# Pairing the first unit's attention tiles into one series and delaying the operand mixing in a fused attention and maxout kernel on Trainium2

## The chip, the cores and the metric

The kernel runs on one core of one Trainium2 chip. The metric is the time of one execution in microseconds (us). The engines are named as in the profile: PE is TensorE, DVE is VectorE, ACT is ScalarE, POOL is GpSimd, SP is SyncE, whose queue issues nearly all DMAs here. PEld is PE's loading of stationary operands.

## The reference, cut to what matters

Chunked softmax attention (8 batches, 8 heads, 576 positions, 64 columns, chunks of 64), and behind it a layer of three matrix products of which the largest is kept, and an output product:

```python
scores = scale * np.matmul(q_c, k_c.transpose(0, 1, 2, 4, 3))
scores = scores - np.max(scores, axis=-1, keepdims=True)
attn = np.exp(scores)
attn = attn / (np.sum(attn, axis=-1, keepdims=True) + 1e-09)
out = np.matmul(attn, v_c)
...
h = np.maximum(np.maximum(x @ w1, x @ w2), x @ w3)   # x 4608x512, w 512x768
return (h @ w_out).astype(np.float32)                # w_out 768x512
```

All of it is float32; the kernel splits each operand of a product into a high and a low part and makes three products (`three`).

## The kernel before, in words

The 4608 rows are 36 tiles of 128. Tiles 0 to 3 are a first group, whose order is written out by hand (`FIRST`). Tiles 4 to 7 are a second group, with plain products. Tiles 8 to 35 are four units of 6, 8, 8 and 6 tiles (`UNITS`). Each unit has a hidden layer of nine sets of seven products each (a fast scheme that needs seven products of half size where eight would stand, in the order `ORDER` = 1, 6, 5, 7, 2, 3, 4), and an output layer (`project`) of 6 x 3 matmuls a tile. A product is six matmuls of 384 columns in units of 6 tiles and of 512 columns in units of 8. The weights of a set (1.75 MB) come back from DRAM into a ring of two places (`load`, two DMAs), where they were put, mixed, during the second group (`store`, `stores`, nine times).

Attention of a tile goes through these steps, named as in the code: q (load of q and k), S (scores, 64x64 matmuls on PE), mx and sub on DVE, exp on ACT, sum, eps, rec on DVE, nrm (the division), T (four transposes on PE), at (copy to SBUF on ACT), v (load), V (values, 64x64 matmuls on PE), x (copy on ACT into `stage`). The attention of a unit is made in the stage before it, and its steps are put between the matmuls there. A clock of planned time, `now`, is moved on by each product (`passed`), and a step planned for a time (`plan`) is issued as soon as `now` has come to it. So the order on each engine is fixed when the program is built, and an engine takes its instructions in that order, waiting at each for its data.

Before the change two ways of placing attention exist. For units 1 to 3 `insertion` takes tiles two by two: the V of one pair and the S of the next stand together on PE, with the offsets of `PAIR` and `PAIR_T`; V writes to two banks of PSUM out of the five that the products use (`take`, `give`), and nrm is on POOL. For the six tiles of the first unit, `attention` and `tiles` place each tile by itself during the second group, with the offsets of `TABLE` and `LATER`; S and V of these tiles write to the two halves of a bank of their own, and nrm is on DVE.

A unit's operands X1 to X7 are made from `stage` during the output layer of the stage before it (`operands`: a cast on ACT as the high part, a difference on DVE as the low part, and four mixing differences, two on DVE and two on POOL), at times counted from the end of the hidden layer, from 0.0 to 9.4, all moved by `OPERANDS`. In the output layer a tile's result is copied out of its bank by ACT (`output`). The parts H of the hidden layer that the output layer reads come from a cast on ACT and a difference on DVE (`high`, `low` of `hidden`); those of the last set are needed in the output layer after its first 36 matmuls and the first tile's next three.

Of the kernel before, what the change touches and what calls it, by code (L numbers as in the profile page):

```python
# [19 lines left out]
B, H, S, D = 8, 8, 576, 64  # L20
P = 128
# [7 lines left out]
STEP, TILE = 0.6815, 2.05  # L29
STEP_H = {6: 0.517, 7: 0.6003, 8: 0.6815}  # L30
ORDER = (1, 6, 5, 7, 2, 3, 4)
TABLE = (("q", -7.0, 0.0), ("v", -1.0, 0.0), ("S", 0.0, 0.7), ("mx", 1.0, 0.0), ("sub", 1.9, 0.0), ("exp", 2.8, 0.0),
         ("sum", 3.8, 0.0), ("eps", 4.7, 0.0), ("rec", 4.9, 0.0), ("nrm", 5.3, 0.0), ("T", 8.0, 0.65), ("at", 8.9, 0.0),
         ("V", 10.6, 0.7), ("x", 11.6, 0.0))
PAIR = (("mx", 1.4, 2.9), ("sub", 2.2, 3.7), ("exp", 3.1, 4.6), ("sum", 4.1, 6.0), ("eps", 5.0, 6.9), ("rec", 5.2, 7.1),
        ("nrm", 5.6, 7.5))
PAIR_T = (("T", 10.0, 12.4, 0.46), ("at", 10.9, 13.3, 0.0))
OPERANDS = 0.3
MIX = 0.5
LATER = {"q": -2.0, "v": 1.5, "T": 1.4, "at": 1.4, "V": 2.8, "x": 2.8}  # L40

# [26 lines left out]
def chunk_attn_maxout_kernel(  # L68
# [10 lines left out]
    nc = tc.nc  # L79
# [134 lines left out]
    def bank_of(name):  # L214
        if name not in banks_of:
            banks_of[name] = ps[name].tile([P, 2, 2, 4, 64], F32, name=name[-1])
        return banks_of[name]

    def plain_steps(t, x_of, col, paired=None):


        st = {}

        def load_qk():
            st["r"] = att.tile([P, 2, 8, 64], F32, name="buf", tag=("raw", "kk", "aa")[t % 3] if t < 8 else ("raw", "kk")[t % 2],
                               bufs=1)
            nc.sync.dma_start(out=st["r"], in_=qk[t])

        def load_v():
            st["v"] = att.tile([P, 8, 64], F32, name="buf", tag=f"vs{t % 2}", bufs=1)  # L230
            nc.sync.dma_start(out=st["v"], in_=vb[t])

        def scores():
            r = st["r"]
            st["s"] = s = bank_of("ps_s")[:, :, t % 2 if t < 4 or paired is not None else 0]
            for g in range(4):
                for h, c in quarters:
                    a, b = halves_of[c], halves_of[h]
                    nc.tensor.matmul(out=s[b, c, g, :], lhsT=r[a, 0, 2 * g + h, :], rhs=r[a, 1, 2 * g + h, :],  # L239
                                     start=True, stop=True)  # L240

        def maximum():
            st["mx"] = tmp.tile([P, 32], F32, name="mx")[:, :8]
            nc.vector.tensor_reduce(out=st["mx"].rearrange("p (g c) -> p c g", c=2), in_=st["s"], axis=AX.X, op=ALU.max)  # L244

        def less():
            st["e"] = ep.tile([P, 4, 2, 64], F32, name="e", tag=("et", "e")[t % 2])
            most = st["mx"].rearrange("p (g c) -> p c g", c=2)
            nc.vector.tensor_tensor(out=st["e"].rearrange("p g c k -> p c g k"), in0=st["s"],  # L249
                                    in1=most.unsqueeze(3).broadcast_to([P, 2, 4, 64]), op=ALU.subtract)  # L250

        def exp():
            nc.scalar.activation(out=st["e"], in_=st["e"], func=AF.Exp, scale=SCALE)

        def total():
            total, st["guard"], st["invert"], st["norm"] = over_sum(st["e"].rearrange("p g c k -> p (g c) k"))
            total()

        def transpose():
            st["tp"] = tp = ps_t.tile([P, 4, P], F32, name="tp")  # L260
            for g in range(4):
                nc.tensor.transpose(out=tp[:, g, :], in_=st["e"][:, g].rearrange("p c k -> p (c k)"),  # L262
                                    identity=ident)

        def transposed():
            st["at"] = xs_p.tile([P, 4, P], F32, name="xs")
            nc.scalar.copy(out=st["at"], in_=st["tp"])

        def values():
            if paired is not None:  # L270
                x = [p[:, t % 2] for p in paired["x"]]
            else:
                st["x"] = bank_of("ps_x")[:, :, t % 2] if t < 4 else bank_of("ps_s")[:, :, 1]
                x = [st["x"][:, c] for c in range(2)]
            for g in range(4):
                for h, c in quarters:
                    a, b = halves_of[c], halves_of[h]
                    nc.tensor.matmul(out=x[c][b, g, :], lhsT=st["v"][a, 2 * g + h, :], rhs=st["at"][a, g, b],  # L278
                                     start=True, stop=True)

        def part(x):
            return x[:, :, col:col + P].rearrange("p g (c x) -> p c g x", c=2)

        def high():
            nc.scalar.copy(out=part(x_of()[0]), in_=st["x"])

        def low():
            xh, xl = x_of()
            nc.vector.tensor_tensor(out=part(xl), in0=st["x"], in1=part(xh).bitcast(F32), op=ALU.subtract)  # L289

        def whole():
            nc.scalar.copy(out=part(x_of()), in_=st["x"])

        return dict(q=load_qk, v=load_v, x=whole, S=scores, mx=maximum, sub=less, exp=exp, sum=total,
                    eps=lambda: st["guard"](), rec=lambda: st["invert"](), nrm=lambda *eng: st["norm"](*eng),
                    T=transpose, at=transposed, V=values, xh=high, xl=low)

    begun = {}

    def attention(t, x_of, col, norm, later):  # L300
        steps = begun[t] if t in begun else plain_steps(t, x_of, col)
        step = steps["nrm"]
        steps["nrm"] = lambda: step(norm)
        return [(at + later.get(name, 0.0), pe, steps[name]) for name, at, pe in TABLE
                if not (t in begun and name == "q")]

    outputs = []

# [367 lines left out]
    def plan(at, pe, fn):  # L676
        heapq.heappush(due, (at, len(order), pe, fn))
        order.append(fn)
# [23 lines left out]
        units.append((unit(t0, count, rooms), t0, count))  # L702
        t0 += count

    def tiles(lead, time):
        _, t0, count = units[0]
        for tt in range(count):
            first = now + lead + (time - 13.5 - lead) * tt / (count - 1)
            for at, pe, fn in attention(t0 + tt, stage, tt * P, nc.vector, LATER):
                plan(first + at, pe, fn)  # L710

    pairs = []
    for _, t0, count in units[1:]:
        for n in range(0, count, 2):
            both = dict(col=n * P)
            both["tiles"] = [plain_steps(t0 + tt, stage, tt * P, both) for tt in (n, n + 1)]
            pairs.append(both)

    def value_banks(both):
# [12 lines left out]
    def insertion(when, k, behind=0.0):  # L732
# [8 lines left out]
        for n, steps in enumerate(scored):  # L741
            plan(when + 0.003 + 0.001 * n, 0.65, steps["S"])
            for name, *at in PAIR:
                fn = steps[name]
                plan(when + lead + at[n], 0.0, (lambda fn=fn: fn(nc.gpsimd)) if name == "nrm" else fn)
# [4 lines left out]
            for n, steps in enumerate(pairs[k + 1]["tiles"]):  # L750
                plan(when + 4.0 + n, 0.0, steps["q"])

    def series(u, time):

        done = sum(count // 2 for _, _, count in units[1:u + 1])
        if u + 1 >= len(units):
            return
        n = units[u + 1][2] // 2
        lead = 9.0
        if u == 0:  # L760
            for m, steps in enumerate(pairs[0]["tiles"]):
                plan(now - 4.0 + m, 0.0, steps["q"])
            plan_at = now + 4.0
            insertion(plan_at, 0)
            lead = 20.0
        for k in range(n):
            insertion(now + lead + (time - 3.5 - lead) * k / (n - 1), done + k + 1, 14.0 if k == n - 1 else 0.0)

# [10 lines left out]
    def operands(u):  # L779
        if u < len(units):  # L780
            for at, fn in units[u][0]["operands"]():
                plan(now + OPERANDS + at, 0.0, fn)

    def load(u, n, *at):
        if n >= len(sets):
# [2 lines left out]
            for t, fn in zip(at, units[u][0]["load"](n)):  # L788
                plan(now + t, 0.0, fn)

    inner = 3 * JT * CT * STEP + UNITS[0] * TILE
    parts += [("do", lambda: tiles(7.0, inner - 2.0))]
    parts += [("steps", lambda j=j, w=w: g["hidden"](j, w)) for j in range(JT) for w in range(3)]
    parts += [("do", change), ("do", lambda: operands(0)), ("do", lambda: load(0, 0, 0.0, 1.0)), ("do", lambda: load(0, 1, 2.0, 3.0))]
    parts += [("steps", lambda: g["project"](0, 1)), ("steps", lambda: g["project"](2)), ("steps", lambda: g["project"](3))]
    def units_of(u):
        return UNITS[u] if u < len(UNITS) else 0

    for u, (it, t0, count) in enumerate(units):
        time = len(sets) * 14 * STEP_H[count] + (units_of(u + 1) * 1.6)  # L800
        parts.append(("do", lambda u=u, time=time: series(u, time)))
        for n in range(len(sets)):
            parts.append(("steps", lambda it=it, n=n: it["hidden"](n)))
            parts.append(("do", lambda u=u, n=n: load(u, n + 2, 0.3, 0.9)))
# [56 lines left out]
```

## Time and profile before

| | |
|---|---|
| median of 3 runs | 637.86 us (637.18 to 639.95) |
| profiled execution | 637.51 us |
| its span, first to last instruction | 635.7 us |
| PE busy | 623.2 us, 98% of the span |
| DVE busy | 415.0 us, 65% |
| ACT busy | 233.9 us, 37% |
| POOL busy | 217.9 us, 34% |
| granted TensorE clock, mean | 1.000 |

Busy time of an engine is counted without its register, branch and semaphore instructions. The profiled execution's time is 1.8 us above its span. Matmuls are pipelined, so one begins before the one ahead of it ends: what a matmul costs is read from the distance of two starts and not from its own duration. The second group lasts from about 95.6 to 174.1 us, unit 0 to 283.2 us, unit 1 to 415.8 us, unit 2 to 541.9 us.

### The profile page before, as it was taken

How to read it: one execution, taken by the hardware profiler on the slowest of the kernel's cores; microseconds unless marked ns; L12 is line 12 of the kernel's file. 1: busy time of each engine (PE TensorE's matmuls, PEld its weight loads, DVE VectorE, ACT ScalarE, POOL GpSimd, SP SyncE). 2: the span in 40 equal slices, each digit the busy share in tenths (PEclk: the TensorE clock that was granted, in tenths of full speed). 3: DMA queues.
4: the chain of work that ended last, by engine and by line, in shares of the span. 5: the costliest groups of instructions: out<-in, count | busy, mean ns of one | idle time of the engine just before them, and what ended most of it. 6: DMA issues, size and time to landing. Idle time of an engine off the chain costs nothing.

```text
span 635.7 us, 12387 instructions
## 1 busy us (share of the span) xinstructions
PE 623.2 (98%) x5101; PEld 530.0 (83%) x5102; DVE 415.0 (65%) x661; ACT 233.9 (37%) x400; POOL 217.9 (34%) x186
## 2 busy tenths in 40 slices
PE   7899999999999999999999999999999999999997
PEld 4888878777899999788888888788888888999986
DVE  5889855886767676956767679336676690376530
ACT  4988633443424333442332324312223151122121
POOL 3423577882332233222332234213232350222210
PEclk9999999999999999999999999999999999999999
DMA  8978559763869774825474817227454162367502
GB/s 331 389 278 289 194 179 332 241 230 143 330 227 321 250 274 174 318 112 196 167 298 148 296 31 309 100 81 285 167 214 168 64 263 85 134 232 246 217 18 82
DMA packets 36055, 133.70 MB, mean 210 GB/s; under 512 B 4000, under 2 KB 6560, under 8 KB 30240
## 3 DMA queue, kind: packets, MB, share of 16 engines
q1 hardware_dynamic: 35856, 132.79, 56.7%
q8 instruction: 40, 0.66, 0.4%
q14 instruction: 15, 0.12, 0.1%
q10 hardware_dynamic: 144, 0.13, 0.1%
HBM read 106.95 MB, written 25.95 MB: 209 GB/s over the span
## 4 chain that ended last, share of the span: by engine, by line
PE 88%; DVE 8%; DMA 1%; POOL 1%; issue 1%; ACT 1%; SPq 0%; ACTq 0%; POOLq 0%; DVEq 0%
PE pm L189 27%; PE pm L190 26%; PE pm L191 26%; PE s L239 3%; PE tp L262 2%; PE pm L278 2%; DMA ring<-w 1%; PE s L278 1%; DVE X L465 1%; DVE most L525 1%; PE pm L638 1%; DVE e L249 1%; DVE sm L197 1%; DVE mx L244 1%; DVE kept L456 1%
## 5 line engine op out<-in xcount | busy, mean ns | idle before, releaser
L189 PE MATMUL pm<-X,ring 128*128 128x512 f32 (+1 forms) x504 | 185.4, 368 | 0.5 <-DVE most L525 0.3
L191 PE MATMUL pm<-X,ring 128*128 128x512 f32 (+1 forms) x504 | 182.5, 362 | 0.0
L190 PE MATMUL pm<-X,ring 128*128 128x512 f32 (+1 forms) x504 | 182.4, 362 | 0.0
L519 POOL TENSOR_TENSOR kept<-kept 128x384 f32<-128x384 f32 (+1 forms) x36 | 41.5, 1152 | 229.1 <-DVE kept L513 218.8
L513 DVE TENSOR_TENSOR kept<-pm,kept 128x384 f32<-128x384 f32 (+1 forms) x72 | 44.8, 622 | 110.6 <-PE pm L191 109.9
L189 PEld LDWEIGHTS pm<-X,ring 128*128 128x128 f32 x504 | 94.6, 188 | 11.5 <-DVE most L525 1.1
L191 PEld LDWEIGHTS pm<-X,ring 128*128 128x128 f32 x504 | 94.6, 188 | 10.0
L190 PEld LDWEIGHTS pm<-X,ring 128*128 128x128 f32 x504 | 94.7, 188 | 9.5
L510 ACT COPY kept<-pm 128x384 f32<-128x384 f32 (+1 forms) x72 | 38.4, 533 | 124.0 <-PE pm L191 116.8
L189 PE MATMUL pm<-woh,H 128*128 128x512 f32 x168 | 66.2, 394 | 2.5 <-DVE H L535 1.4
L190 PE MATMUL pm<-wol,H 128*128 128x512 f32 x168 | 65.5, 390 | 0.0
L191 PE MATMUL pm<-woh,H 128*128 128x512 f32 x168 | 65.5, 390 | 0.0
L189 PE MATMUL pm<-xh,wl 128*128 128x512 f32 (+1 forms) x156 | 61.0, 391 | 0.0
L190 PE MATMUL pm<-xl,wh 128*128 128x512 f32 (+1 forms) x156 | 58.4, 374 | 0.3 <-DVE xl L289 0.3
L191 PE MATMUL pm<-xh,wh 128*128 128x512 f32 (+1 forms) x156 | 58.4, 374 | 0.0
L206 POOL TENSOR_TENSOR e<-e,sm 128x512 f32<-128x512 f32 x27 | 30.3, 1124 | 74.4 <-DVE sm L203 73.6
L516 DVE TENSOR_TENSOR pm<-pm,kept 128x384 f32<-128x384 f32 (+1 forms) x72 | 45.3, 629 | 14.3 <-PE pm L191 14.1
L525 DVE TENSOR_TENSOR most<-pm,most 128x384 f32<-128x384 f32 (+1 forms) x72 | 44.9, 624 | 2.1
L531 ACT CAST H<-most 128x384 fp32r<-128x384 f32 (+1 forms) x48 | 27.0, 568 | 40.7 <-DVE most L525 40.7
L244 DVE TENSOR_REDUCE mx<-s 128x8 f32<-128x512 f32 x36 | 24.6, 685 | 25.1 <-PE s L239 25.1
L189 PEld LDWEIGHTS pm<-woh,H 128*128 128x128 f32 x168 | 31.5, 188 | 9.7 <-DVE H L535 1.8
L191 PEld LDWEIGHTS pm<-woh,H 128*128 128x128 f32 x168 | 31.5, 188 | 6.7
(94 smaller groups left out, 949.7 us busy)
## 6 DMA issues: line engine op xcount, KB each, us to landing
ring<-w SPq DMA_DIRECT2D x36, 1024.0 KB, 7.1
ring<-w SPq DMA_DIRECT2D x36, 768.0 KB, 4.4
buf<-in_qk SPq DMA_DIRECT2D x36, 512.0 KB, 5.7
buf<-in_vb SPq DMA_DIRECT2D x36, 256.0 KB, 6.1
w<-s SPq DMA_DIRECT2D x9, 1024.0 KB, 4.8
out_x<-ao SPq DMA_DIRECT2D x35, 256.0 KB, 2.0
stage<-in_w SPq DMA_DIRECT2D x7, 512.0 KB, 4.6
xl<-in_w SPq DMA_DIRECT2D x5, 512.0 KB, 7.5
```

The costliest lines, as they stand in the source:

```text
L189: nc.tensor.matmul(out=o, lhsT=al, rhs=bh, start=first, stop=False)
L190: nc.tensor.matmul(out=o, lhsT=ah, rhs=bl, start=False, stop=False)
L191: nc.tensor.matmul(out=o, lhsT=ah, rhs=bh, start=False, stop=last)
L206: eng.tensor_tensor(out=e, in0=e, in1=sm.unsqueeze(2).broadcast_to([P, 8, 64]), op=ALU.mult)
L239: nc.tensor.matmul(out=s[b, c, g, :], lhsT=r[a, 0, 2 * g + h, :], rhs=r[a, 1, 2 * g + h, :], start=True, stop=True)
L244: nc.vector.tensor_reduce(out=st["mx"].rearrange("p (g c) -> p c g", c=2), in_=st["s"], axis=AX.X, op=ALU.max)
L510: return lambda: nc.scalar.copy(out=kept(k), in_=o[i])
L513: return lambda: nc.vector.tensor_tensor(out=kept(k), in0=o[i], in1=kept(q), op=plus)
L516: return lambda: nc.vector.tensor_tensor(out=o[i] if w else M(j, c), in0=o[i], in1=kept(k), op=plus)
L519: nc.gpsimd.tensor_tensor(out=kept(2), in0=kept(2), in1=kept(1), op=plus)
L525: return lambda: nc.vector.tensor_tensor(out=M(j, c), in0=of(), in1=M(j, c), op=most)
L531: nc.scalar.copy(out=hh[j][:, c * half:(c + 1) * half], in_=M(j, c))
```

## The change

The first unit's tiles go by pairs too. `attention`, `tiles`, `TABLE` and `LATER` are gone; `pairs` now holds the pairs of all four units, and `series(0, ...)` places the first unit's three pairs, and the S of unit 1's first pair, during the second group. nrm of the first unit stays on DVE (`both["norm"]`). The operands of units 1 to 3 are begun 2.0 after the end of the hidden layer and not 0.3, and their times are stretched by 1.8; those of unit 0 stay where they were.

```diff
-OPERANDS = 0.3
+OPERANDS, SLOWER = (0.3, 2.0), (1.0, 1.8)
...
-    for _, t0, count in units[1:]:
+    for u, (_, t0, count) in enumerate(units):
         for n in range(0, count, 2):
-            both = dict(col=n * P)
-            both["tiles"] = [plain_steps(t0 + tt, stage, tt * P, both) for tt in (n, n + 1)]
+            both = dict(col=n * P, norm=nc.gpsimd if u else nc.vector)
+            both["tiles"] = [begun[t] if t in begun else plain_steps(t, stage, (t - t0) * P) for t in (t0 + n, t0 + n + 1)]
+            for steps in both["tiles"]:
+                steps["pair"](both)
             pairs.append(both)
...
-    def series(u, time):
-
-        done = sum(count // 2 for _, _, count in units[1:u + 1])
-        if u + 1 >= len(units):
-            return
-        n = units[u + 1][2] // 2
-        lead = 9.0
-        if u == 0:
-            for m, steps in enumerate(pairs[0]["tiles"]):
-                plan(now - 4.0 + m, 0.0, steps["q"])
-            plan_at = now + 4.0
-            insertion(plan_at, 0)
-            lead = 20.0
+    def series(u, time, lead):
+
+        done = sum(count // 2 for count in UNITS[:u])
+        n = UNITS[u] // 2 if u < len(UNITS) else 0
+        if u == 0:
+            insertion(now + 3.0, 0)
         for k in range(n):
             insertion(now + lead + (time - 3.5 - lead) * k / (n - 1), done + k + 1, 14.0 if k == n - 1 else 0.0)
...
-                plan(now + OPERANDS + at, 0.0, fn)
+                plan(now + OPERANDS[min(u, 1)] + SLOWER[min(u, 1)] * at, 0.0, fn)
...
-    inner = 3 * JT * CT * STEP + UNITS[0] * TILE
-    parts += [("do", lambda: tiles(7.0, inner - 2.0))]
+    inner = 3 * JT * CT * STEP + UNITS[0] * 1.65
+    parts += [("do", lambda: series(0, inner, 18.0))]
...
-        time = len(sets) * 14 * STEP_H[count] + (units_of(u + 1) * 1.6)
-        parts.append(("do", lambda u=u, time=time: series(u, time)))
+        time = len(sets) * 14 * STEP_H[count] + 1.65 * sum(UNITS[u + 1:u + 2])
+        parts.append(("do", lambda u=u, time=time: series(u + 1, time, 12.0 if u == 0 else 9.0)))
```

PE, second group, before: the S of a tile (out `s`, x16) and the T of another (out `tp`) stand as two pieces of their own between the products.

```order
L191 MATMUL pm<-xh,wh_116 128x512
L239 MATMUL s<-buf 64x64 x16
L189 MATMUL pm<-xh,wl_122 128x512
L190 MATMUL pm<-xl,wh_116 128x512
L191 MATMUL pm<-xh,wh_116 128x512
L262 MATMUL tp<-ident,e 128x128 x4
```

PE, second group, the change: V of two tiles (out `pm` from `xs`) and S of the next two (line 274 for V and 235 for S, which were 278 and 239).

```order
L187 MATMUL pm<-xh,wh_115 128x512
L274 MATMUL pm<-xs,buf 64x64 x32
L235 MATMUL s<-buf 64x64 x32
L185 MATMUL pm<-xh,wl_122 128x512
L186 MATMUL pm<-xl,wh_116 128x512
L187 MATMUL pm<-xh,wh_116 128x512
```

From the second group to the end of the attention, six S and six V of one tile (x16 each) are gone from PE, and ten pieces of V and S of two tiles each (x32 and x32) have become thirteen; the one S of a lone pair (x32), which stood in unit 0, now stands at the second group's start.

DVE, start of the output layer of unit 0, before: operands X1 (here X_1983) and X2 (X_1993) and the mixing difference (out `kept`) stand ahead of the last three H.

```order
L465 TENSOR_TENSOR X_1983<-stage,X_1983 128x1024
L200 TENSOR_SCALAR sm<-sm 128x8
L203 RECIPROCAL sm<-sm 128x8
L525 TENSOR_TENSOR most<-kept,most 128x384
L456 TENSOR_TENSOR kept<-stage 128x1024
L535 TENSOR_TENSOR H<-most,H 128x384
L197 TENSOR_REDUCE sm<-e 128x8
L465 TENSOR_TENSOR X_1993<-stage,X_1993 128x1024
L200 TENSOR_SCALAR sm<-sm 128x8
L535 TENSOR_TENSOR H<-most,H 128x384
L203 RECIPROCAL sm<-sm 128x8
L535 TENSOR_TENSOR H<-most,H 128x384
```

DVE, the same place, the change: X1 is X_2036; the lines are 454 for X, 524 for H, 445 for the mixing difference, 193 for sum.

```order
L514 TENSOR_TENSOR most<-kept,most 128x384
L245 TENSOR_TENSOR e<-s,mx 128x2x4x64
L193 TENSOR_REDUCE sm<-e 128x8
L196 TENSOR_SCALAR sm<-sm 128x8
L199 RECIPROCAL sm<-sm 128x8
L454 TENSOR_TENSOR X_2036<-stage,X_2036 128x1024
L524 TENSOR_TENSOR H<-most,H 128x384 x2
L193 TENSOR_REDUCE sm<-e 128x8
L196 TENSOR_SCALAR sm<-sm 128x8
L445 TENSOR_TENSOR kept<-stage 128x1024
```

The mixing difference, one sum and X2's low part, which stood ahead of the last two H, now stand behind them; X1's low part still stands ahead.

ACT, output layer of unit 1, before: all seven casts of operands stand ahead of the first copy of a result (`ao`).

```order
L461 CAST X_2010<-kept 128x1024
L461 CAST X_2027<-kept 128x1024
L461 CAST X_2033<-stage 128x1024
L461 CAST X_2043<-stage 128x1024
L461 CAST X_2059<-kept 128x1024
L566 COPY ao<-pm 128x512 x5
```

ACT, the same place, the change: the casts are line 450, the copies line 555.

```order
L450 CAST X_2077<-kept 128x1024
L450 CAST X_2097<-kept 128x1024
L555 COPY ao<-pm 128x512
L450 CAST X_2103<-stage 128x1024
L555 COPY ao<-pm 128x512
L450 CAST X_2113<-stage 128x1024
L555 COPY ao<-pm 128x512
L450 CAST X_2129<-kept 128x1024
L555 COPY ao<-pm 128x512 x2
```

The first three copies of results now stand ahead of the last cast.

## Rows read from the trace of the kernel before

**Rows 1.** The page, busy time by engine: us (share of the span) xinstructions
```profile
PE 623.2 (98%) x5101; PEld 530.0 (83%) x5102; DVE 415.0 (65%) x661; ACT 233.9 (37%) x400; POOL 217.9 (34%) x186
```

**Rows 2.** Waits of PE: us in total, times, longest
```profile
PE pm L189 <- DVE H L535: 1.4, 1, 1.4
PE pm L189 <- ACT ao L566: 1.1, 1, 1.1
PE s L239 <- issue: 1.1, 1, 1.1
...
PE pm L189 <- DVE most L525: 0.3, 1, 0.3
PE pm L189 <- DMA ring<-w: 0.2, 1, 0.2
```

**Rows 3.** Timeline of PE, second group: start us, us, what
```profile
99.72 0.39 PE L189 MATMUL pm<-xh,wl 128*128 128x512 f32 x1
...
102.89 0.39 PE L191 MATMUL pm<-xh,wh 128*128 128x512 f32 x1
103.21 0.69 PE L239 MATMUL s<-buf 64*64 64x64 f32 x32
...
104.64 0.39 PE L189 MATMUL pm<-xh,wl 128*128 128x512 f32 x1
...
115.97 0.39 PE L191 MATMUL pm<-xh,wh 128*128 128x512 f32 x1
116.28 0.69 PE L278 MATMUL s<-xs,buf 64*64 64x64 f32 x32
...
117.72 0.39 PE L189 MATMUL pm<-xh,wl 128*128 128x512 f32 x1
```

**Rows 4.** Timeline of PE, unit 0
```profile
194.72 0.34 PE L191 MATMUL pm<-X,ring 128*128 128x384 f32 x1
194.99 1.16 PE L278 MATMUL pm<-xs,buf 64*64 64x64 f32 x64
195.97 1.11 PE L239 MATMUL s<-buf 64*64 64x64 f32 x64
...
197.65 0.33 PE L189 MATMUL pm<-X,ring 128*128 128x384 f32 x1
...
205.79 0.34 PE L191 MATMUL pm<-X,ring 128*128 128x384 f32 x1
```

**Rows 5.** Timeline of DVE, output layer of unit 0
```profile
261.68 1.95 DVE L456 TENSOR_TENSOR kept<-stage 128x1024 f32<-128x1024 f32 x1
...
264.02 0.67 DVE L197 TENSOR_REDUCE sm<-e 128x8 f32<-128x512 f32 x1
264.61 1.21 DVE L465 TENSOR_TENSOR X<-stage,X 128x1024 fp32r<-128x1024 f32 x1
```

**Rows 6.** Timeline of ACT, output layer of unit 1; idle time before it in brackets
```profile
400.88 1.05 ACT L461 CAST X<-kept 128x1024 fp32r<-128x1024 f32 x1 [4.54 <-POOL kept L456]
```

**Rows 7.** Chain that ended last, unit 0: start us, us, what
```profile
182.86 0.33 SPq L476
...
183.72 8.36 DMA ring<-w
...
215.27 1.05 issue
```

**Rows 8.** Timeline of SP: last store of mixed weights
```profile
153.10 0.33 SPq L428 DMA_DIRECT2D w<-s  x1
```

**Rows 9.** Timeline of ACT, second group's end
```profile
158.52 0.83 ACT L461 CAST X<-stage 128x768 fp32r<-128x768 f32 x1 [1.55 <-DMA w<-s]
159.26 0.61 ACT L347 CAST h<-m 128x512 fp32r<-128x512 f32 x1
```

**Rows 10.** Timeline of DVE, second group's end
```profile
160.26 0.68 DVE L350 TENSOR_TENSOR h<-m,h 128x512 fp32r<-128x512 f32 x1
```

More of the change, by code (lines that the diff above doesn't have):

```diff
@@ L31 @@
 ORDER = (1, 6, 5, 7, 2, 3, 4)
-TABLE = (("q", -7.0, 0.0), ("v", -1.0, 0.0), ("S", 0.0, 0.7), ("mx", 1.0, 0.0), ("sub", 1.9, 0.0), ("exp", 2.8, 0.0),
-         ("sum", 3.8, 0.0), ("eps", 4.7, 0.0), ("rec", 4.9, 0.0), ("nrm", 5.3, 0.0), ("T", 8.0, 0.65), ("at", 8.9, 0.0),
-         ("V", 10.6, 0.7), ("x", 11.6, 0.0))
 PAIR = (("mx", 1.4, 2.9), ("sub", 2.2, 3.7), ("exp", 3.1, 4.6), ("sum", 4.1, 6.0), ("eps", 5.0, 6.9), ("rec", 5.2, 7.1),
@@ L37 @@
 PAIR_T = (("T", 10.0, 12.4, 0.46), ("at", 10.9, 13.3, 0.0))
-OPERANDS = 0.3
+OPERANDS, SLOWER = (0.3, 2.0), (1.0, 1.8)
 MIX = 0.5
-LATER = {"q": -2.0, "v": 1.5, "T": 1.4, "at": 1.4, "V": 2.8, "x": 2.8}
 FIRST = """
@@ L217, in bank_of, with plain_steps @@
         return banks_of[name]
-    def plain_steps(t, x_of, col, paired=None):
+    def plain_steps(t, x_of, col):
         st = {}
@@ L234, in scores @@
             r = st["r"]
-            st["s"] = s = bank_of("ps_s")[:, :, t % 2 if t < 4 or paired is not None else 0]
+            st["s"] = s = bank_of("ps_s")[:, :, t % 2 if t < 4 or "pair" in st else 0]
             for g in range(4):
@@ L269, in values @@
         def values():
-            if paired is not None:
-                x = [p[:, t % 2] for p in paired["x"]]
+            if "pair" in st:
+                x = [p[:, t % 2] for p in st["pair"]["x"]]
             else:
@@ L289, in low, with pair @@
             nc.vector.tensor_tensor(out=part(xl), in0=st["x"], in1=part(xh).bitcast(F32), op=ALU.subtract)
-        def whole():
-            nc.scalar.copy(out=part(x_of()), in_=st["x"])
-        return dict(q=load_qk, v=load_v, x=whole, S=scores, mx=maximum, sub=less, exp=exp, sum=total,
+        def pair(both):
+            st["pair"] = both
+        return dict(q=load_qk, v=load_v, pair=pair, S=scores, mx=maximum, sub=less, exp=exp, sum=total,
                     eps=lambda: st["guard"](), rec=lambda: st["invert"](), nrm=lambda *eng: st["norm"](*eng),
@@ L298, in chunk_attn_maxout_kernel @@
     begun = {}
[L300 to L305, printed above, removed]
     outputs = []
@@ L703, in chunk_attn_maxout_kernel @@
         t0 += count
[L705 to L710, printed above, removed]
     pairs = []
-    for _, t0, count in units[1:]:
+    for u, (_, t0, count) in enumerate(units):
         for n in range(0, count, 2):
-            both = dict(col=n * P)
-            both["tiles"] = [plain_steps(t0 + tt, stage, tt * P, both) for tt in (n, n + 1)]
+            both = dict(col=n * P, norm=nc.gpsimd if u else nc.vector)
+            both["tiles"] = [begun[t] if t in begun else plain_steps(t, stage, (t - t0) * P) for t in (t0 + n, t0 + n + 1)]
+            for steps in both["tiles"]:
+                steps["pair"](both)
             pairs.append(both)
@@ L744, in insertion @@
                 fn = steps[name]
-                plan(when + lead + at[n], 0.0, (lambda fn=fn: fn(nc.gpsimd)) if name == "nrm" else fn)
+                plan(when + lead + at[n], 0.0, (lambda fn=fn: fn(pairs[k]["norm"])) if name == "nrm" else fn)
             for name, *at, pe in PAIR_T:
@@ L795, in chunk_attn_maxout_kernel @@
     parts += [("steps", lambda: g["project"](0, 1)), ("steps", lambda: g["project"](2)), ("steps", lambda: g["project"](3))]
-    def units_of(u):
-        return UNITS[u] if u < len(UNITS) else 0
     for u, (it, t0, count) in enumerate(units):
-        time = len(sets) * 14 * STEP_H[count] + (units_of(u + 1) * 1.6)
-        parts.append(("do", lambda u=u, time=time: series(u, time)))
+        time = len(sets) * 14 * STEP_H[count] + 1.65 * sum(UNITS[u + 1:u + 2])
+        parts.append(("do", lambda u=u, time=time: series(u + 1, time, 12.0 if u == 0 else 9.0)))
         for n in range(len(sets)):
```

## The prediction

> **What bounds the kernel now.** I began with the page. PE is busy for 623.2 us [rows 1] of a span of 635.7, at full granted clock throughout (mean 1.000), so its stream of matmuls is the bound and a change must either shorten that stream or remove a wait in it. The view of waits comes next: behind the start-up, PE waits only a few times [rows 2]. 1.4 us went to an H that DVE made late, 1.1 to a bank that ACT copied late, 1.1 to "issue", 0.3 to a bank that DVE read late, 0.2 to a ring load. They sum to 4.1 us. All else must come from the stream.
>
> What the stream costs is read from starts. Fifteen 512-column matmuls begin from 99.72 to 102.89 [rows 3], so one takes (102.89 - 99.72) / 14 = 0.226 us. Forty-eight 384-column ones begin from 197.65 to 205.79 [rows 4], so one takes 8.14 / 47 = 0.173. Against this I hold the places where attention is put in. Around the S of a lone tile four steps lie from 102.89 to 104.64 [rows 3], which is 1.75 us where four products take 0.91: a lone S costs 0.84. The V of a lone tile, 115.97 to 117.72 [rows 3], costs the same 0.84. Around V and S of a pair, four steps lie from 194.72 to 197.65 [rows 4], 2.93 us where four products take 0.69: four tiles' worth of small matmuls cost 2.24, or 0.56 each. Pairing is cheaper by 0.28 for each S or V.
>
> **The change part by part.** *The pairs.* The order shows that six lone S and six lone V go, and that ten paired pieces of V and S become thirteen; one S of a lone pair stands on both sides and cancels, as do all the T. That removes 12 x 0.84 = 10.1 us and adds 3 x 2.24 = 6.7, so 3.4 us less on the engine that is the bound. Two of the three new pieces stand among 512-column products where the row that I price from has 384; the starts ahead of and behind the piece are counted out, so I take the same price. Nothing hides on PE, so this term stands unless a wait comes in.
>
> *What the pairs wait for.* nrm of this unit was on DVE and stays there, so DVE's work in the second group is the same, only bunched; PE's T of the second tile of a pair comes after two sets of mx, sub, sum and nrm. I take no wait: below it is zero, and above I bound it by the longest wait of PE for DVE in these rows, 1.4 us [rows 2], once in the second group. V now takes two of the five banks there. A product of the second group fills a bank for 12 x 0.226 = 2.7 us, so the three others are enough as long as DVE is not a whole bank late; the bound is the 0.3 of such a wait [rows 2], and I take zero.
>
> *The second group's end comes sooner.* Before it, 10.1 us of lone S and V stand in the second group; behind the change three pieces of 2.24 and the pair of S, which costs about half a piece, stand in it: some 8 us. So the hidden layer ends about 2 us earlier, while the mixing of the weights goes on at its own pace on POOL, ACT and DVE. Its last store is issued at 153.10 [rows 8], and ACT's cast of X1, which takes that store's room, waits for it 1.55 us until 158.52 [rows 9]. Behind that cast stand on ACT the cast of h at 159.26 [rows 9], and on DVE h at 160.26, done at 160.9 [rows 10], which PE needs after the first 30 matmuls of the output layer, 30 x 0.226 = 6.8 us after its start. The second group ends at 174.1 with an output layer of 72 x 0.226 = 16.3 us, which so began at 157.8; h was wanted at 164.6, so 3.7 us were spare; with the end 2 us sooner about 1.6 are. On DVE the sub and sum of unit 1's first pair now stand ahead of it too, though mostly before the cast ends. I take no wait and keep the bound for the rivals.
>
> *Operands of units 1 to 3.* In the output layer of unit 0 the mixing difference of 1.95 us, a sum of 0.67 and X2's low part of 1.21 [rows 5] stood on DVE ahead of the H for which PE waited 1.4 [rows 2]. In the new order all three, 3.8 us, stand behind it. Against this the last V and S of unit 0 come nine matmuls later, 9 x 0.173 = 1.6 us, and with them mx and sub. 3.8 - 1.6 = 2.2 is more than 1.4, so this wait goes: -1.4.
>
> In the output layer of unit 1 ACT stood idle for 4.54 us before its last cast, for a mixing difference of POOL [rows 6], with the copies of results behind it; PE waited 1.1 us [rows 2] for the first of those copies. In the new order three copies stand ahead of that cast: -1.1. What is late instead are X4 and X7: planned at 9.4 before, at 2.0 + 1.8 x 9.4 = 18.9 now. The output layers take 6 x 18 x 0.226 = 24.4 us in unit 0 and 8 x 18 x 0.226 = 32.5 in the others of 8 tiles, and ORDER wants X4 last, six products further on. So the delay costs nothing.
>
> *The ring in unit 0.* A set there takes 42 x 0.173 = 7.3 us and what is put in. The tightest load ran from its first issue at 182.86 to 183.72 + 8.36 = 192.08 [rows 7], 9.2 us, and PE waited 0.2 for it [rows 2]. Set by set I put the new insertions in: the sets with one T only, the shortest, go from three to two, but these two now follow each other, and one of their loads shares the queue with q and v of a pair. I keep 0.2 as it is; bounds 0 and, at 9.2 - 7.7 = 1.5 each for the two sets, less the 1.0 by which a set's second load is wanted later than its start, 1.0 in all.
>
> *The issue wait.* PE stood for 1.05 us in the midst of one paired piece's S at 215.27 [rows 7], with nothing to wait for that the profile shows. One of ten paired pieces had it. I keep it, once, as 1.1 [rows 2]. The Trainium skill, Runtime: NRT & Kernel Launch, section "Instruction fetch mechanics", says that an engine's instructions are fetched in blocks of 256 and that the cost of crossing into the next is mostly hidden. The trace agrees for nine pieces of ten and not for the tenth; by the rule alone the three new pieces would cost nothing, and a paired piece, with its 128 matmul records [rows 4], would be the place where hiding is hardest.
>
> **Sum.** 637.5 (the profiled execution) - 3.4 - 1.4 - 1.1 = 631.6 us. The median of the runs is 0.35 above the profiled execution, well inside their own spread of 2.8, so I leave it out.
>
> **Rivals.** *A, the waits move.* The pieces are cheaper, but bunched DVE work gives back a wait as long as those that go (in T of the second group or at its end). For it: ACT and DVE take instructions in a fixed order, and both waits that go were of that kind; the margins above are 0.8 (unit 0) and 1.6 us (second group's end). Against it: at the two old places the order now has the culprit behind. Then only 3.4 stays: 634.1.
>
> *B, issue waits come with the pieces.* For it: the one wait lay in such a piece, and there are three more. Against it: nine of ten had none. If all three have one, 631.6 + 3 x 1.1 = 634.9.
>
> *C, the mixed weights fall behind, slower.* If the bunched DVE work delays the mixing so that its last store lands a period later, ACT's cast of X1, h and PE's output layer all wait for it. The stores are planned 7.2 us apart in the code, the last issued at 153.10 [rows 8]. With 1.6 us spare, each further microsecond costs one: a full period costs 5.6, which gives 637.2, and it decides from 1.6 + 5.9 = 7.5 us of lateness on, where the whole gain is gone. Two periods, 14.4, would give 631.6 + 12.8 = 644.4. Against it: DVE is busy for 65% of the span [rows 1], and its operations in the second group do not grow in number before the last pair.
>
> *D, all waits go,* the issue, ring and bank waits too, since their places move: 631.6 - 1.1 - 0.2 - 0.3 = 630.0, and half a microsecond less where the matmul behind a wait, which starts slowly, runs at its usual pace.
>
> **How the numbers follow.** The forecast has 0.55, D 0.20, A 0.11, B 0.08, C 0.06. The likeliest gives 631.6. From the unknown costs its own range is 630.0 to 633.6 (below as D, above 1.4 + 0.3 + 0.8 more waits, less what is unlikely at once). The range to hold 8 in 10 reaches from 629.3 to 634.6, over D's lower end and A, and leaves B's top and C out. About 0.5% of 637.9, 3.2 us, is what a measurement of this kernel can tell from no change: faster is below 634.7. The forecast, D and most of A lie there, 0.85; same has the rest of A, B and a C of about one period, 0.12; slower has a C of two periods, 0.03.
>
> **What would show it.** Right: in the view of waits the H of line 524 and the copy of line 555 are gone from PE's list; paired pieces in the second group cost 2.2 to 2.3 us by starts; PE's busy time falls by about 3.4, the span by about 6. The second group's hidden layer ends near 155.5. Wrong: a wait of PE's T (line 258) for DVE in the second group (A); several issue waits at lines 235 or 274 (B); ACT's cast at line 450 waiting for a store until after 161, with PE's output layer behind it (C); PE waiting for the ring in several sets of unit 0.

## The result and the profile after

The changed kernel takes 631.01 us (median of 4 runs, 630.58 to 631.44) where the kernel before takes 637.87 (4 runs beside it, 637.18 to 639.95): a ratio of 0.9887, 95% interval 0.9863 to 0.9912. The profiled execution took 631.41 us with a span of 629.6, so 6.1 us less than before's on either count. The forecast was 631.6. The total was met; of the steps behind it some were met and some were not, and their errors nearly cancel, which is luck.

The page after, busy time by engine, answers to [rows 1]:

```profile
PE 619.9 (98%) x5102; PEld 529.9 (84%) x5102; DVE 415.3 (66%) x661; ACT 233.5 (37%) x400; POOL 218.4 (35%) x186
```

The waits of PE after (us in total, times, longest), against [rows 2]:

```profile
...
PE pm L627 <- DVE h L629: 1.2, 1, 1.2
PE x L274 <- ACT xs L263: 0.7, 1, 0.7
PE x L274 <- issue: 0.6, 1, 0.6
PE tp L258 <- DVE e L202: 0.6, 1, 0.6
...
```

None of the five rows of [rows 2] stands in this view any more: H, the copy of a result, the issue wait in unit 0, the bank and the ring (the ring's wait is only shorter, see the account of the steps). The 1.2 and the 0.7 belong to the start-up and were there before. New are 0.6 of issue, in the first group, and 0.6 in which a T (line 258) waits for DVE's division: rival A's kind of wait, at rival A's place.

Where the 6.1 us came from is read stage by stage. The windows of before, each from the first matmul of a stage to the first of the next (columns: window, its length, then busy time and instructions of PE and PEld, DVE, ACT, POOL, the granted clock, DMA share, GB/s), for the second group's hidden layer, unit 0's hidden layer, its output layer, and unit 1 whole:

```profile
95.64:157.75 62.11, 62.11 (x626) 48.65 (x624) 44.57 (x60) 26.24 (x40) 41.26 (x42) 1.00 0.66 240
174.07:256.02 81.95, 80.42 (x987) 77.56 (x986) 56.28 (x116) 27.58 (x54) 26.54 (x26) 1.00 0.69 245
256.02:283.15 27.13, 25.78 (x118) 20.96 (x117) 22.81 (x25) 12.64 (x19) 8.96 (x4) 1.00 0.62 242
283.15:415.82 132.67, 131.57 (x1067) 108.58 (x1066) 87.30 (x130) 42.55 (x69) 39.59 (x28) 1.00 0.51 189
```

The same four after:

```profile
97.12:158.09 60.97, 60.35 (x690) 49.32 (x688) 46.54 (x63) 26.46 (x41) 41.89 (x42) 1.00 0.68 257
174.41:252.94 78.53, 78.42 (x924) 76.47 (x922) 53.87 (x108) 26.43 (x52) 24.26 (x24) 1.00 0.64 234
252.94:278.39 25.45, 25.45 (x118) 21.06 (x117) 22.87 (x25) 12.72 (x19) 10.30 (x4) 1.00 0.67 258
278.39:409.68 131.29, 131.29 (x1067) 108.64 (x1066) 88.36 (x130) 42.76 (x70) 39.64 (x28) 1.00 0.50 191
```

The stages shrink by 1.14, 3.42, 1.68 and 1.38 us, 7.6 together; all others agree within 0.05. Against this the second group begins 1.48 later, at 97.12 and not 95.64. The order of PE's instructions is the same up to that place, and over all profiles of this study, of either order, it begins between 95.0 and 97.1; the eleven of the new order alone fill that whole range. So this is taken as a difference of executions that belongs to neither kernel; 0.6 of it is the issue wait in the first group. 7.6 - 1.5 gives the 6.1.

The price of the pieces, from a timeline of PE in the second group (start us, us, what), to be read like [rows 3] and [rows 4]:

```profile
115.71 0.39 PE L187 MATMUL pm<-xh,wh 128*128 128x512 f32 x1
116.03 1.16 PE L274 MATMUL pm<-xs,buf 64*64 64x64 f32 x64
117.01 1.11 PE L235 MATMUL s<-buf 64*64 64x64 f32 x64
118.05 0.50 PE L185 MATMUL pm<-xh,wl 128*128 128x512 f32 x1
...
118.86 0.39 PE L185 MATMUL pm<-xh,wl 128*128 128x512 f32 x1
```

Four products and a paired piece lie from 115.71 to 118.86, 3.15 us; less 4 x 0.2265 that is 2.24, the price that was read from unit 0.

### The profile page after: what moved, and what is told of

It is laid out like the page before. It is cut to its first block, busy times and chain, and to the rows that moved or that the text cites. A ratio compares the mean times of both kernels' runs of the same rounds, so it can differ in the third digit from the quotient of the medians.

```text
span 629.6 us, 12374 instructions
## 1 busy us (share of the span) xinstructions
PE 619.9 (98%) x5102; PEld 529.9 (84%) x5102; DVE 415.3 (66%) x661; ACT 233.5 (37%) x400; POOL 218.4 (35%) x186
## 4 chain that ended last, share of the span: by engine, by line
PE 92%; DVE 6%; ACT 1%; issue 1%; POOL 0%; DVEq 0%; ACTq 0%; POOLq 0%
PE pm L185 28%; PE pm L186 28%; PE pm L187 28%; PE s L235 2%; PE pm L274 2%; PE tp L258 2%; PE pm L627 1%; DVE e L245 1%; DVE s L406 1%; DVE sm L193 1%; DVE mx L240 1%; DVE sm L196 0%; POOL c L398 0%; DVE m L329 0%; DVE xl L285 0%
## 5 line engine op out<-in xcount | busy, mean ns | idle before, releaser
L202 POOL TENSOR_TENSOR e<-e,sm 128x512 f32<-128x512 f32 x27 | 32.2, 1194 | 80.4 <-DVE sm L199 49.5
```

The lines of the kernel that those rows point to most:

```text
L202: eng.tensor_tensor(out=e, in0=e, in1=sm.unsqueeze(2).broadcast_to([P, 8, 64]), op=ALU.mult)
```

## The experiments

Times are medians with the lowest and highest run, ratios are against the kernel before on the same chip, and lengths of stages are read as above.

**The pairs alone, the operands alone.** In the first, the operands are where they were before, and all else of the change stays, its smallest number too (see the third run):

```diff
-OPERANDS, SLOWER = (0.3, 2.0), (1.0, 1.8)
+OPERANDS, SLOWER = (0.3, 0.3), (1.0, 1.0)
```

> The changed kernel with the operands of units 1 to 3 begun at 0.3 and not stretched, as before the change: the pairs alone. My theory (pairs 3.4 us of PE's stream, operands 1.4 + 1.1 us of two waits, the two independent): 637.9 - 3.4 = about 634.0 with the ring, bank and issue waits in their new places, 2.5 above the changed kernel; PE waits again for an H in unit 0's output layer and for a copy ao in unit 1's. Rival (the later operands do nothing once the last pair has moved to the end of unit 0): 631 to 631.5 and no such waits.

Measured: 631.99 us (630.25 to 633.29), ratio 0.9913 [0.9891, 0.9935]. The H wait did not come back: that H was done 8.59 us after the start of unit 0's output layer, where PE wants it at 8.88 (10.34 in the kernel before), so 0.3 was to spare. Unit 1 took 131.29 us as in the changed kernel, with no wait for a copy. Instead unit 0's output layer took 26.65 and not 25.45, since there a copy was late. From the view of waits:

```profile
PE pm L185 <- ACT ao L555: 0.9, 1, 0.9
```

ACT in that output layer, idle time in brackets:

```profile
273.52 1.05 ACT L450 CAST X<-kept 128x1024 fp32r<-128x1024 f32 x1 [3.69 <-POOL kept L445]
274.47 2.04 ACT L555 COPY ao<-pm 128x512 f32<-128x512 f32 x4
```

It is the pattern of [rows 6], a cast that waits for POOL's mixing with four copies queued behind it, in another unit. So with the pairs in place the edit of the operands is worth 1.2 us there, and nothing in unit 1.

In the second, the kernel before gets the later and slower operands and nothing else:

```diff
-OPERANDS = 0.3
+OPERANDS, SLOWER = (0.3, 2.0), (1.0, 1.8)
...
-                plan(now + OPERANDS + at, 0.0, fn)
+                plan(now + OPERANDS[min(u, 1)] + SLOWER[min(u, 1)] * at, 0.0, fn)
```

> The kernel before the change with the later and slower operands of units 1 to 3 alone. My theory: 637.9 - 2.5 = 635.4, without the two waits of PE for H and ao, and the lone S and V at 0.84 each as before. Rival (the waits only move to the next place, or the first unit's tiles and the operands need each other): 637 to 638.

Measured: 634.82 (632.00 to 635.55), ratio 0.9950 [0.9931, 0.9968]. Both waits are gone: unit 0's output layer takes 25.50 and unit 1 131.29, 3.0 us less than before together. By itself this edit does what the two terms, 1.4 + 1.1, said.

**The number of the series alone** (the third run). The diff holds one more edit, of which the prediction says nothing: 1.6 us a tile becomes 1.65 in the length over which a series is spread. Here it is put into the kernel before by itself:

```diff
-        time = len(sets) * 14 * STEP_H[count] + (units_of(u + 1) * 1.6)
+        time = len(sets) * 14 * STEP_H[count] + (units_of(u + 1) * 1.65)
```

> The kernel before the change with one number of the change alone: the series of units 1 to 3 reckons 1.65 us of planned time for a tile to come, not 1.6. In the order this puts the V and S at the head of unit 1's output layer three matmuls later, and on POOL both mixing differences of unit 2's operands now stand ahead of both nrm, where before they took turns. With the pairs alone PE did not wait in unit 1's output layer, though the operands were as early as before. Theory: that wait of 1.1 us (1.3 with its slow start) hangs on POOL's order and goes with this number alone: unit 1's two layers fall from 132.7 to 131.3 us. In unit 0 POOL's turns now go nrm, mixing, nrm, mixing, as they did in unit 1 before, so PE may wait for a copy ao there, about 1 us, in the place of the 1.4 for H. Rival, that of my prediction (the wait goes only with later operands): unit 1 stays at 132.7.

Measured: 638.39 (637.62 to 639.85), ratio 1.0013 [0.9998, 1.0028], no change that can be told. Inside, two things moved against each other, unit 1 by -1.4 and unit 0's output layer by +2.8 us. Unit 1 takes 131.28, so its wait for the copy went by this edit alone. POOL in unit 1's output layer, before:

```profile
390.09 1.83 POOL L206 TENSOR_TENSOR e<-e,sm 128x512 f32<-128x512 f32 x1 [11.92 <-DVE sm L203]
...
397.48 3.37 POOL L456 TENSOR_TENSOR kept<-stage,kept 128x1024 f32<-128x1024 f32 x1
```

and with the number changed, where the mixing stands ahead of the divisions and not behind them:

```profile
395.40 2.41 POOL L456 TENSOR_TENSOR kept<-stage,kept 128x1024 f32<-128x1024 f32 x1 [6.55 <-DVE X L465]
399.38 1.82 POOL L206 TENSOR_TENSOR e<-e,sm 128x512 f32<-128x512 f32 x1 [1.57 <-ACT ao L566]
```

The mixing is done at 397.81 and not at 400.85, and the cast on ACT that waits for it, with the copies behind, is 3.03 us earlier (397.85 where [rows 6] have 400.88), although the output layer there began 0.1 us later. In unit 0's output layer the same edit makes the H wait longer, 2.6 us where [rows 2] have 1.4:

```profile
PE pm L189 <- DVE H L535: 2.6, 1, 2.6
...
PE s L239 <- issue: 1.7, 1, 1.7
```

The layer takes 29.97 us, 4.5 more than without a wait, because the granted clock fell behind this one (last section). The gain in unit 1 and the loss in unit 0 don't touch each other: unit 1's wait can be removed by either edit, but only once.

**Later or slower.** The changed kernel with one half of the edit of the operands, one execution each.

```diff
-OPERANDS, SLOWER = (0.3, 2.0), (1.0, 1.8)
+OPERANDS, SLOWER = (0.3, 2.0), (1.0, 1.0)
```

> The changed kernel with the operands of units 1 to 3 begun at 2.0 and not stretched. In unit 0's output layer ACT has one copy ao ahead of its last cast, and the last two H of DVE have only X1 and a mixing difference ahead of them. Theory: the beginning alone is enough there, 25.5 us as in the changed kernel, where the pairs alone took 26.7. If the stretching is what takes the wait away, PE waits about 1 us and it takes 26.5.

Measured: 631.34 us.

```diff
-OPERANDS, SLOWER = (0.3, 2.0), (1.0, 1.8)
+OPERANDS, SLOWER = (0.3, 0.3), (1.0, 1.8)
```

> The changed kernel with the operands of units 1 to 3 stretched by 1.8 and begun at 0.3. Three copies ao stand ahead of ACT's last cast in unit 0's output layer, as in the changed kernel. Theory: enough too, 25.5 us. If the beginning counts, PE waits for an H or an ao, 26.5.

Measured: 629.82 us. In both, unit 0's output layer takes 25.45 and unit 1 131.29, exactly as with both halves: either half is enough. Both together only add room, since the fourth H is ready at 260.71 in a layer that begins at 252.94, and with the later start alone at 261.62 in one that begins at 252.85, 1.0 us later against the layer's start. The 1.5 us between the two executions lie in unit 0's hidden layer, 79.74 and 78.26, where PE's order is the same in both; in the first PE waited 1.1 for the ring, in the second not at all. That is a difference of executions.

**V and S of each pair apart.** The changed kernel with 2.5 us between the V of one pair and the S of the next:

```diff
-        lead = 1.0 * bool(k)
+        lead = 3.5 * bool(k)
...
-            plan(when + 0.003 + 0.001 * n, 0.65, steps["S"])
+            plan(when + 2.5 * bool(k) + 0.003 + 0.001 * n, 0.65, steps["S"])
```

> The changed kernel with the S of a pair put 2.5 us of planned time behind the V of the pair ahead of it, and all that follows S moved by as much: thirteen pieces of V and S fall into 26. If what pairing saves is a price that each entry into small matmuls has (a lone pair's S cost 1.30 and V and S of a pair together 2.24, so 2 x 1.30 - 2.24 = 0.36 each), 13 x 0.36 = 4.7 us more than the changed kernel, some 635.7. If the price hangs on the number of small matmuls alone, no change: 631.

Measured: 637.35 (636.76 to 638.60), ratio 0.9998 [0.9984, 1.0012]: the whole gain is gone. PE in the second group:

```profile
117.54 0.40 PE L187 MATMUL pm<-xh,wh 128*128 128x512 f32 x1
117.87 1.16 PE L235 MATMUL s<-buf 64*64 64x64 f32 x64
118.96 0.50 PE L185 MATMUL pm<-xh,wl 128*128 128x512 f32 x1
...
119.76 0.40 PE L185 MATMUL pm<-xh,wl 128*128 128x512 f32 x1
```

The S of a pair by itself costs 119.76 - 117.54 - 4 x 0.2265 = 1.31 us, and the V by itself the same. Together they cost 2.24, so each further change from 128x128 products to 64x64 ones and back costs 0.38; thirteen of them are 5.0 us of the 7.7 by which the stages from the second group on grew in this profile (6.3 by the medians). Most of the rest are T that wait for ACT:

```profile
PE tp L258 <- ACT xs L263: 2.1, 3, 1.5
```

The Trainium skill, TensorEngine Tiling (Array Packing), section "Key Properties", says that changing the tiling mode drains TensorE. It gives no price; these rows agree with it and give 0.38 us for going in and out once, but that a drain is what the 0.38 pays for is not shown.

**The wait of T.** In the changed kernel the T that waits stands in the second group; PE there, idle time in brackets:

```profile
145.00 0.39 PE L187 MATMUL pm<-xh,wh 128*128 128x512 f32 x1
146.01 0.63 PE L258 MATMUL tp<-ident,e 128*128 128x128 f32 x4 [0.62 <-DVE e L202]
```

DVE ahead of it, with a division that took 1.62 us where the median of its kind is 0.69:

```profile
143.26 0.70 DVE L196 TENSOR_SCALAR sm<-sm 128x8 f32<-128x8 f32 x1
144.00 0.20 DVE L199 RECIPROCAL sm<-sm 128x8 f32<-128x8 f32 x1
144.24 1.62 DVE L202 TENSOR_TENSOR e<-e,sm 128x512 f32<-128x512 f32 x1
```

First, both T of each pair in the second group, and their copies, 1.2 us later:

```diff
-                plan(when + lead + behind + at[n], pe, steps[name])
+                plan(when + lead + behind + 1.2 * (k < 3) + at[n], pe, steps[name])
```

> The changed kernel with the T of the first unit's pairs planned 1.2 us later. In the changed kernel's trace PE waits 0.6 us, with its slow start behind it 0.8, for DVE's nrm at one T of the second group, and loses 0.2 at another. If that wait is only a T put too soon, both go and the time falls by about 1.0, to 630.0. If DVE's work is late altogether there, the wait moves to the V behind it, and the time stays at 631.

Measured: 633.16 (631.98 to 633.96), ratio 0.9930 [0.9907, 0.9952]; the second group's hidden layer grew from 60.97 to 62.81. The wait for the division is gone and a longer one came: 2.4 us in two T for ACT. ACT there, with PE's second T of the pair starting at 130.94:

```profile
128.83 0.62 ACT L336 CAST h<-m 128x512 fp32r<-128x512 f32 x1 [5.25 <-DVE m L329]
129.36 1.04 ACT L403 CAST s<-c 128x1024 fp32r<-128x1024 f32 x1
130.31 0.58 ACT L263 COPY xs<-tp 128x512 f32<-128x512 f32 x1
```

By moving the copy too, the cast of h and a cast of weights came ahead of it on ACT, and the copy of the first T frees the bank that the second T needs. So two versions move T and leave the copy where it is: the first T of each pair only, and both.

```diff
-                plan(when + lead + behind + at[n], pe, steps[name])
+                plan(when + lead + behind + 0.6 * (k < 3 and n == 0 and name == "T") + at[n], pe, steps[name])
```

> The changed kernel with T of the first tile of each of the first unit's pairs three matmuls later, its copy on ACT and all else where they were. The run with both T 1.2 us later made the copy of the first T fall behind a cast of h on ACT, and PE waited there. Theory: with the copy kept ahead of that cast, the wait of 0.8 us at the T of the third pair goes, and the second group's hidden layer falls from 61.0 to about 60.1 us. Rival (DVE is late as a whole): the second T waits instead, and it stays at 61.0.

Measured: 629.95 (628.86 to 630.65), ratio 0.9886 [0.9866, 0.9906]; that hidden layer takes 60.61.

```diff
-                plan(when + lead + behind + at[n], pe, steps[name])
+                plan(when + lead + behind + 0.6 * (k < 3 and name == "T") + at[n], pe, steps[name])
```

> The changed kernel with both T of each of the first unit's pairs 0.6 us later in planned time and their copies where they were: one product later for the first T of all three pairs and for the second T of the last two. With the first T alone moved, PE's wait at the third pair's first T fell from 0.8 to 0.2, and 0.3 came at the second. Theory: that 0.3 goes, and the second group's hidden layer falls to 60.2 us from 60.6 (61.0 in the changed kernel): 0.8 us under the changed kernel in that stretch, 630.2 by time. Rival: the second T's copy falls behind on ACT and V waits for it, 60.6 or more.

Measured: 629.87 (629.36 to 630.65), ratio 0.9873 [0.9858, 0.9888], and 60.31. The slow division is still there, of 1.62 us again, and PE waits for it no more, because a product lies between. Beside the first of these two the changed kernel ran once more, unchanged:

> The changed kernel once more, beside the next three on one chip. Its stretches between the second group's start and the end should be those of the first look within 0.5 us each (where no instruction wait falls into one); the time ahead of the second group, where nothing was changed and 1.5 us more stood than in the kernel before, should come out between the two (95.6 to 97.1 us), which makes it a difference of executions. If the change itself had cost something there, it stays at 97.

Measured: 630.84 (629.00 to 632.06), ratio 0.9900 [0.9876, 0.9923], stages within 0.15 us of the first profile. The intervals overlap, so by their medians alone the two versions can't be told from it; by the stage that was edited they are 0.4 and 0.7 us shorter, in one profile each. The second has the shortest such stage of all kernels here; that it is the fastest is not shown.

**Rival C, the mixing behind.** The mixing and its stores are planned 3 us later:

```diff
-MIX = 0.5
+MIX = 3.5
```

> The changed kernel with the mixing of all weights planned 3.0 us later. The last store then lands about 3 us later. In the changed kernel h was done 1.9 us before PE wanted it. If the store is what ACT's first cast of an operand, then h, then PE wait for, as in my rival C, PE waits 3.0 - 1.9 = 1.1 us for an h at the start of the second group's output layer, and the time rises by that, to 632. If the mixing has more room than I read from the rows (or the store comes no later, since the engines set its pace and not the plan), no change: 631.

Measured: 631.56 (631.09 to 631.68), ratio 0.9911 [0.9889, 0.9933], 0.7 above the changed kernel run beside it. In the changed kernel ACT's cast of X1 begins after the store at 160.26, h is ready at 162.97, and PE wants it at 158.09 + 6.8 = 164.9: 1.9 us to spare, where 1.6 were forecast. With the mixing later ACT reads

```profile
161.12 0.84 ACT L450 CAST X<-stage 128x768 fp32r<-128x768 f32 x1 [2.90 <-DMA w<-s]
...
162.40 0.61 ACT L336 CAST h<-m 128x512 fp32r<-128x512 f32 x1
```

and DVE's h is done at 163.83, wanted at 157.71 + 6.8 = 164.5: 0.7 to spare. The store landed 3.0 us later against the group's start (66.0 where it was 63.0), but the layer grew by 1.74 meanwhile, since T waited for what the mixing had been moved into:

```profile
PE tp L258 <- DVE e L202: 1.2, 2, 0.7
PE tp L258 <- ACT xs L263: 0.8, 1, 0.8
```

The lateness is paid at the T's first, and that itself gives the store more time. Another run puts all divisions of the first unit on POOL, which mixes too:

```diff
-            both = dict(col=n * P, norm=nc.gpsimd if u else nc.vector)
+            both = dict(col=n * P, norm=nc.gpsimd)
```

> The changed kernel with nrm of the first unit's tiles on POOL, as in the other units. POOL's chain of mixing gets six more operations of about 1.2 us, 7 us in all. If that chain has no room, the last store lands up to 7 us later, PE waits some 5 us at the end of the second group, and besides at T for nrm: 634 to 638. If POOL's idle time takes them up (it waited 1.2 to 2.9 us for DVE in each period), the time stays at 631, or falls by the 0.8 us of PE's wait for nrm on DVE.

Measured: 633.52 (631.74 to 634.90), ratio 0.9942 [0.9920, 0.9963]; the waits at T for POOL grew from 1.9 us (start-up) to

```profile
PE tp L258 <- POOL e L202: 4.3, 4, 1.9
```

and the hidden layer to 63.62, with the store 4.3 us later against the group's start and h still 0.3 us in time.

## Why the prediction came out, step by step

**The pairs, -3.4: right.** Every piece after costs what was read from before, and 12 x 0.84 of lone pieces against 3 x 2.24 gives the 3.4. (All three new pieces stand among 512-column products, not two; the price is the same.) Pulling V and S apart showed why: the number of small matmuls is the same, and nine fewer changes between large and small products, at 0.38 each, are the 3.4.

**The operands, -1.4 and -1.1: right by themselves, wrong as terms on top of the pairs.** "At the two old places the order now has the culprit behind" was true, and the runs show 3.0 us where 2.5 were put down (the windows lost 1.68 and 1.38 to waits that the view of waits has as 1.35 and 1.10). But in the changed kernel these 3.0 do not belong to that edit alone. Unit 1's wait goes already by 1.65 in place of 1.6, of which the prediction says nothing. The H wait does not come back when the operands are put back, since the new series has other work ahead of H on DVE, with 0.3 us to spare; what comes back is 1.2 us of another wait. Both the sum and its sign were right; the attribution was wrong because each edit was weighed against the old order, not against the order with the other edits in.

**"T: I take no wait": wrong by about 1 us.** A T waited for DVE's division at 146.01 (0.8 by starts, 0.62 in the view of waits), and one at 113.36 lost 0.2 by starts. That is rival A, within the bound of 1.4 that the text gave. The bound looked at how much work DVE has; what happened is that the same work took longer. The division of 1.62 us ran beside a mixing operation of POOL at 144.02, and the neighbours stretched as well.

**Issue and bank kept, 1.4: wrong, they went; the ring kept, 0.2: it stayed.** By starts the three had cost 2.2 us in unit 0's hidden layer, 1.8 of them issue and bank. Those two cost nothing there after, which is rival D for them. The ring still costs 0.3 after, with 0.11 of idle time, too little for the view of waits: a load landed at 201.47, and the product that reads it starts 0.45 us behind the one ahead, where 0.17 is usual.

```profile
201.16 0.34 PE L187 MATMUL pm<-X,ring 128*128 128x384 f32 x1
201.61 0.41 PE L185 MATMUL pm<-X,ring 128*128 128x384 f32 x1
```

How much the ring costs is a matter of executions. With PE's order the same the view of waits has none in one and 1.1 in another, and six of the eleven profiles with the new placement have 0.4 to 1.1. Why the issue wait went is not shown; where it can be is told below.

**Rival C: the margin was right,** 1.9 us where 1.6 was worked out, but partly by luck: the hidden layer shrank by 1.1 and not 2, and h came 0.5 later against the group's start, where no change was reckoned with. And the rival's mechanism, each microsecond of lateness costing one, was not seen. In both runs that made the store late, the price came earlier, at T.

**The sum.** Issue and bank waits that went (1.4 in the sum, 1.8 by starts) and slow starts of 0.5 were too little gain; T waits of 1.0 and a start that happened to be 1.5 us later were not in it. Together these would make the execution 0.2 later than the forecast. It came 0.2 earlier, 631.4 for 631.6, so some 0.4 us have no term here. That errors of up to 1.8 us came so near to cancelling is luck. Had the second group begun where it did before, they would have shown as 1.5 us more gain, 629.9, at the forecast's own lower end.

**The signs.** H and the copy are gone from PE's list, a piece in the second group costs 2.24, PE's busy time fell by 3.3 and the span by 6.1, as was said. But the second group's hidden layer ended at 158.09 and not near 155.5, since it began 1.5 later and its T lost 1.0.

## What to carry to other kernels

Read the price of a small inserted piece from starts, and count how often the stream changes between large and small matmuls; that term was exact. Weigh every edit of a change against the order that all the others make, the smallest number too, since two edits can remove the same wait and a wait is removed only once. Where a step waits for a result, leave a product's room between them, and move the step without the copy that frees its bank.

## What had not been expected of the hardware

**A wait of 2.6 us took the clock down.** With the number of the series alone, PE stood still for 2.60 us ahead of 267.03. The windows of 3 us behind it (columns as above; the granted clock is the third figure from the end):

```profile
267.00:270.00 3.00, 2.97 (x8) 2.37 (x9) 2.96 (x5) 0.27 (x1) 1.15 (x1) 0.56 0.96 388
270.00:273.00 3.00, 3.00 (x13) 2.42 (x12) 3.00 (x3) 2.68 (x3) 2.09 (x1) 0.87 0.05 17
273.00:276.00 3.00, 3.00 (x15) 2.49 (x14) 3.00 (x2) 1.67 (x3) 1.30 (x1) 1.00 0.00 0
```

0.56 is near the lower of the two levels, 1.2 of 2.4 GHz: eight matmuls start in 3 us and not 13, and the wait cost 4.5 us in all. Behind the 1.35 us of the same wait in the kernel before, the granted clock stayed at 1.00, and so it did behind the longest other wait, 1.91 us at a T of the run with all divisions on POOL. The fall was no chance of one execution: all ten of this kernel have a mean clock of 0.996 or 0.997, where nearly all others have 0.999 or 1.000. A wait's length in the view of waits is therefore not always its price.

**The issue wait has few places.** In all three kernels with the old placement (before, the operands alone, the number alone) it stands at the same matmul, after the 59th of an S in unit 0, about 2,113 matmuls from the start. The operands alone, PE:

```profile
214.82 1.09 PE L239 MATMUL s<-buf 64*64 64x64 f32 x59
...
217.43 0.33 PE L239 MATMUL s<-buf 64*64 64x64 f32 x5 [1.51 <-issue]
```

Its size varies: 1.05, 1.51 and 1.68 us. In the eleven profiles with the new placement there is none in the units. Six of these, the changed kernel's among them, have one of 0.4 to 0.7 at about 25 us, always after the 23rd matmul of the same V in the first group. A seventh, with the mixing 3 us later, has one in an earlier V, after the 26th:

```profile
15.46 0.68 PE L274 MATMUL x<-xs,buf 64*64 64x64 f32 x26
16.50 0.34 PE L274 MATMUL x<-xs,buf 64*64 64x64 f32 x6 [0.36 <-issue]
```

So the same few places come back, and the length differs between executions; what decides whether and where such a wait comes is not shown. It fits what the Trainium skill, Runtime: NRT & Kernel Launch, section "Instruction fetch mechanics", says of blocks of instructions fetched one after another, but that the fetch is the cause was not shown by a run here.

**DVE slows beside POOL.** The division went from 0.69 to 1.62 us beside POOL's operations of 512 columns, of which the first ended at 145.31:

```profile
144.02 2.98 POOL L385 TENSOR_TENSOR f<-wh,wl 128x512 f32<-128x512 f32 x2
```

With the number of the series changed X's low part took 2.80 us where [rows 5] have 1.21, beside a mixing of POOL of 2.68 us:

```profile
262.74 2.68 POOL L456 TENSOR_TENSOR stage<-stage 128x1024 f32<-128x1024 f32 x1
263.71 2.80 DVE L465 TENSOR_TENSOR X<-stage,X 128x1024 fp32r<-128x1024 f32 x1
```

DVE's instructions grew by 0.93 and 1.59 us, about what POOL's still had to run when they began, 1.07 and 1.71. The Trainium skill, SBUF — State Buffer, section "Who interferes with whom", says that a DVE instruction with two SBUF inputs contends with a POOL instruction that reads SBUF, for a port that only one of them has at a time; the rows agree with it.
